# Split products with fewer parts: two of y and h, three of the weights, in a scan followed by a maxout layer

## The chip, the cores and the metric

The kernel runs on one core of a Trainium2 chip. The metric is the device time of one execution in microseconds (us), as the median of several timed runs. A separate execution is recorded by the hardware profiler; it has a time of its own, and its trace is what the views of the profile below are made from. Engines are named as the profile names them: PE is TensorE (PEld its weight loads), DVE is VectorE, ACT is ScalarE, POOL is GpSimd, SP is SyncE, which issues most DMAs.

## The reference

First comes a state-space scan (batch 4, 8 heads, 768 positions, head size 32, state size 16), in chunks. Cut to what matters, for one chunk:

```python
L = exp(cum[i] - cum[j]) * causal                  # decay inside the chunk
y_intra = (C B^T * L) x
y_inter = (C state) * exp(cum)
y = y_intra + y_inter
state = exp(sum(la)) * state + sum_j B_j x_j * exp(cum[-1] - cum[j])
```

Its result is turned into a matrix x of 3072 tokens by 256, and a maxout layer follows, in full float32 accuracy, with weights of 256 x 768 (w1, w2, w3) and 768 x 256 (w_out):

```python
h = maximum(maximum(x @ w1, x @ w2), x @ w3)
out = h @ w_out
```

## The kernel before

**Algebra.** With w2 as a base, the kernel makes the differences d0 = w1 - w2 and d1 = w3 - w2, and uses max(x w1, x w2, x w3) = x w2 + max(0, x d0, x d1). The base is folded ahead of time into one matrix, fold = w2 w_out, so that out = x fold + max(0, x d0, x d1) w_out. An "up" product is x times 128 columns of d0 or d1; a "down" product is 128 rows of h times w_out, or x (called y in the code) times fold.

**Split products.** TensorE multiplies the short type fp32r in one pass, and float32 in several. From block 1 on, each operand is therefore split into fp32r parts, and a product is the sum of three products of parts, accumulated in one PSUM bank, with z = 0, 1, 2 as the index of the term. In the kernel before, every operand has three parts: H (near part: the value times a factor close to 1, rounded), L (far part: made from the difference between the value and H) and S (a crossed part made of H and L). The term z is part z of one operand times part z of the other: H H', L L', S S'. The factors NEAR, RAISE and STRETCH are chosen so that the three add up to the full product.

- For y (`scan_y`): ScalarE writes H from PSUM, VectorE writes L as y - H (step `far`), and VectorE writes S by `crossed`, two steps.
- For h (`halve`, `cross_next`): ScalarE writes H, GpSimd writes L as h - H, and VectorE writes S by `crossed`, one up product later.
- For the weights (`split_steps`), four steps: ScalarE writes H; GpSimd (for fold, which lies in PSUM, VectorE) writes a remainder `rest`; ScalarE casts `rest` into S; VectorE writes L from `rest` and the source. There are ten such splits of 128 x 512 elements: six of d0 and d1 in three column pairs, three of w_out, one of fold.

**Blocks.** The tokens are worked in 6 blocks of 512 (4 batches of 128 positions). For each block the scan makes y by many small matmuls (`scan_old`, line 633, and `scan_own`, line 648), then 12 up products u = 0 to 11 follow (line 802, 6 matmuls of 512 columns each), and the down products (line 926, 24 terms of 4 matmuls of 256 columns). u = 2f takes d0 and u = 2f + 1 takes d1 for the column group f; up product u uses the weight pair q = u // 4. After an even u, ScalarE copies the bank to m; after an odd u, VectorE makes h = max(0, bank, m) (`late`). The up products turn between two PSUM banks, so the next but one waits for that copy or that h. Block 0 is made with the unsplit float32 weights while these are decoded (lines 200 to 215) and the differences are made (line 754).

**Order.** The program is scheduled by hand: each engine runs its instructions in the order in which the code issues them. A word plan gives that order. `OPENING` stands for block 0; then each row of `FIRST`, `STEADY` or `LAST` belongs to one up product. `Z` issues the up product, then the split of the last h (`halve`), then the copy or maximum of the product before (`late`). The other words put work between: `buQ:N` takes N steps from the list of weight splits of pair Q (`paired` interleaves those of d0 and d1), `bo:N` from those of w_out, a number N pops N postponed steps (`later`: score weights, y's parts, state sums), `d` issues one down term, `g` and `G` make the folded matrix (the last `G4` also splits it, all steps at once), `r` is the base product of block 0 (line 907), `t`, `c`, `e`, `s`, `A`, `y`, `X`, `W`, `E` are steps of the next block's scan, with masks on GpSimd (line 476). Thus the plan of block 1 (`FIRST`) carries the weight splits beside the up products that need them: pair 1 from u = 4, pair 2 from u = 8. Output blocks are copied from PSUM into `ob` by ScalarE and VectorE (`put`) and stored by SyncE.

Of the kernel before, what the change touches and what calls it, by code (L numbers as in the profile page):

```python
# [12 lines left out]
F32R = mybir.dt.float32r  # L13
AF = mybir.ActivationFunctionType
ALU = mybir.AluOpType
# [5 lines left out]
def kernel(  # L21
# [20 lines left out]
    nc = tc.nc  # L42

    NB, NH, S, D = x.shape
    N = B.shape[-1]
    P = 128
    NC = S // P
    HN = NH * N
# [6 lines left out]
    KD = DM // P  # L55
    NF = DF // P
    BLK = NB * P
# [3 lines left out]
    HB = BLK // 2  # L61
    Q = P // 2
    NU = NF * 2
    NEAR = 1.0 - 2.0 ** -13
    RAISE = 2.0 ** 12
    STRETCH = 1.0 + 1.0 / RAISE
    NFETCH = 8
    MASKED = -32768.0

# [10 lines left out]
    def half(shape, name, dtype=FP32):  # L80

        return halves.tile(shape, dtype, tag="half", name=name)

    def whole(shape, name, dtype=FP32):

        return wholes.tile(shape, dtype, tag="whole", name=name)

    def plain(t):
        return t.bitcast(FP32)
# [7 lines left out]
    def up_bank(shape, name):  # L97
        return bank("up", 2, shape, name)
# [18 lines left out]
    for k in range(REP):  # L117
        eng = nc.sync if k % 2 == 0 else nc.scalar
# [4 lines left out]
        out=a_sb,  # L123
        in_=a_rows.rearrange("r (c i) -> (r c) i", i=P).rearrange("(w r) i -> r w i", w=2))
# [115 lines left out]
    for _ in range(NFETCH):  # L240
# [7 lines left out]
        out=pick, in_=ident.rearrange("p (r k) -> p k r", k=BH), op=ALU.add, axis=AX.X)  # L248
    npick = const.tile([P, BH], FP32, name="npick")
    nc.vector.tensor_scalar(  # L250
        out=npick, in0=pick, scalar1=-1.0, scalar2=None, op0=ALU.mult)
# [4 lines left out]
        out=hsel, in_=hsel, pattern=[[-N, NH]], compare_op=ALU.is_ge, fill=0.0,  # L256
        base=0, channel_multiplier=1)
    nc.gpsimd.affine_select(
        out=hsel, in_=hsel, pattern=[[N, NH]], compare_op=ALU.is_ge, fill=0.0,
# [3 lines left out]
        out=parity, in_=hsel.rearrange("p (r g) -> p g r", g=2), op=ALU.add, axis=AX.X)  # L263
# [6 lines left out]
        out=mask, in_=mask, pattern=[[1, P]], compare_op=ALU.is_ge, fill=MASKED,  # L270
# [10 lines left out]
        out=ind, in_=by_tile[:, :, :, 0:3].rearrange("p t h q -> p h q t"),  # L281
        op=ALU.add, axis=AX.XY)
# [142 lines left out]
    rest = half([R, 2, P], "sums_rest")  # L425
# [108 lines left out]
    def scan_state(c, kind):  # L534
        st = blocks[c]
        A = kind([HN, NB, 2, D], "A")
        for b in range(NB):
            for r in range(NP):
# [6 lines left out]
                    skip_group_check=True)  # L545
        return lambda: own_state(A, "S", (c + 1, 0))

    def own_state(A, name, key):
        states[key] = to = att.tile([HN, NB, 2, D], FP32, tag="S", bufs=5, name=name)
        nc.vector.tensor_tensor(  # L550
            out=to, in0=A,
            in1=parity.unsqueeze(1).unsqueeze(3).to_broadcast([HN, NB, 2, D]), op=ALU.mult)

    def half_states(c):
# [13 lines left out]
        def add(g):  # L568
            to = (c, 1) if g == 0 else (c + 1, 0)
            own_state(As[g], "S", to)  # L570
            old = att.tile([HN, NB, 2 * D], FP32, tag="old", name="old")
# [98 lines left out]
    y_parts = {}  # L670

    def scan_y(c):

        y_parts[c] = tuple(whole([P, KD, BLK], "y" + n, F32R) for n in "HLS")
        H, L, S = y_parts[c]

        def of(t, k, g):
            return t[:, k].rearrange("p (b g i) -> p b g i", b=NB, g=2)[:, :, g]

        ys = blocks[c]["y"]  # L680
        for k in range(KD):
            for g in range(2):
                nc.scalar.mul(of(H, k, g), ys[k][g], NEAR)

        def far(k):
            for g in range(2):
                nc.vector.tensor_tensor(
                    out=of(L, k, g), in0=ys[k][g], in1=of(plain(H), k, g), op=ALU.subtract)

        steps = [lambda k=k: far(k) for k in range(KD)]  # L690
        return steps + [
            lambda k=k: crossed(S[:, k], plain(H)[:, k], plain(L)[:, k]) for k in range(KD)]

    def crossed(out, H, L):
        nc.vector.scalar_tensor_tensor(  # L695
            out=out, in0=L, scalar=-RAISE, in1=H, op0=ALU.mult, op1=ALU.add)

    h0 = {}

# [28 lines left out]
    up_parts, down_parts, fold_parts = {}, {}, []  # L728

    def split_steps(src, parts):  # L730

        shape = [P, 2, WCOL]
        H, L, S = (half(shape, "w" + n, F32R) for n in "HLS")
        rest = half(shape, "rest")
        parts += [H, L, S]
        eng = nc.gpsimd if src.space != PSUM else nc.vector
        return [
            lambda: nc.scalar.mul(H, src, NEAR * STRETCH),  # L740
            lambda: eng.tensor_tensor(out=rest, in0=src, in1=plain(H), op=ALU.subtract),
            lambda: nc.scalar.copy(out=S, in_=rest),
            lambda: nc.vector.scalar_tensor_tensor(  # L743
                out=L, in0=rest, scalar=RAISE, in1=src, op0=ALU.mult, op1=ALU.add),
        ]

    differences = {}
# [1 line left out]
    def up_steps(q, i):  # L749
        state = {}  # L750

        def differ():
            state["d"] = differences[q, i] = d = half([P, 2, WCOL], "d")
            nc.gpsimd.tensor_tensor(  # L754
                out=d, in0=w_raw[DIFF[i]][q], in1=w_raw[BASE][q], op=ALU.subtract)

        def nth(n):
            def step():
                if n == 0:
                    up_parts[q, i] = []  # L760
                    state["rest"] = split_steps(state["d"], up_parts[q, i])
                state["rest"][n]()
            return step

        return [differ] + [nth(n) for n in range(4)]

    def wo_steps(o):
        state = {}

        def nth(n):  # L770
            def step():
                if n == 0:
                    down_parts[o] = []
                    state["rest"] = split_steps(wo_raw[o], down_parts[o])
                state["rest"][n]()
            return step

        return [nth(n) for n in range(4)]

    def paired(one, two):  # L780
        order = (0, 0, 1, 2, 1, 3, 4, 2, 3, 4)
        which = (0, 1, 0, 0, 1, 0, 0, 1, 1, 1)
        return [(one, two)[w][o] for w, o in zip(which, order)]

    later = []
# [5 lines left out]

    held = {}
    h_parts = {c: {} for c in range(NC)}
    opened, crossings = [], []

    def up(c, u):
        f, i = divmod(u, 2)
        q, g = divmod(f, 2)
        held["up"] = bank = up_bank([P, BLK], "up")
        for z in (0, 1, 2):  # L800
            for k in range(KD):
                nc.tensor.matmul(  # L802
                    out=bank, lhsT=up_parts[q, i][z][:, k, g * P:(g + 1) * P],
                    rhs=y_parts[c][z][:, k], start=(z == 0 and k == 0),
                    stop=(z == 2 and k == KD - 1), skip_group_check=True)
        opened.append((c, u, bank))

    def late():
        if not opened:
            return  # L810
        c, u, up = opened.pop(0)
        f, i = divmod(u, 2)
        if i == 0:
            held["m"] = m = half([P, BLK], "m")
            nc.scalar.copy(out=m, in_=up)  # L815
            cross_next()
            return
        h = half([P, BLK], "h")
        nc.vector.scalar_tensor_tensor(  # L819
            out=h, in0=up, scalar=0.0, in1=held["m"], op0=ALU.max, op1=ALU.max)  # L820
        held["h"] = c, f, h

    def halve():

        if "h" not in held:
            return
        c, f, h = held.pop("h")
        H, L = (half([P, BLK], "h" + n, F32R) for n in "HL")
        h_parts[c][f] = [H, L]
        nc.scalar.mul(H, h, NEAR)  # L830
        nc.gpsimd.tensor_tensor(out=L, in0=h, in1=plain(H), op=ALU.subtract)  # L831
        crossings.append((c, f))

    def cross_next():
        if not crossings:
            return
        c, f = crossings.pop(0)
        H, L = h_parts[c][f]
        S = half([P, BLK], "hS", F32R)
        crossed(S, plain(H), plain(L))  # L840
        h_parts[c][f].append(S)

    based = {"T": [], "turned": 0}

# [72 lines left out]
    def pair_of(c, term, z):  # L917
        kind, n = term
        if kind == "y":
            return y_parts[c][z][:, n], fold_parts[z][:, n]  # L920
        return h_parts[c][n][z], down_parts[n // 2][z][:, n % 2]

    def products(c, o, term, z, bs, first):
        left, right = pair_of(c, term, z)
# [116 lines left out]
    for q in range(NQ):  # L1041
        back["u%d" % q] = paired(up_steps(q, 0), up_steps(q, 1))
# [7 lines left out]
    def first_group(n):  # L1050
# [50 lines left out]
        "Z X0 E bu1:2 E load q",  # L1101
        "Z bu1:2 g q g",
        "Z t bu1:2 g q",
        "Z c e 1 bu1:2 q G4",
        "Z X2 E bu2:2 E G4",
        "Z A 1 1 bu2:2 bo:2 G4",
        "Z s 1 bu2:2 bo:2",
        "Z 1 1 bu2:2 bo:2",
        "Z 1 bo:2 r",
        "Z bo:4 r r",  # L1110
        "Z y 1 r d d 2 d",
        "Z W0 E d 2 E d d",
    ]
    STEADY = [
        "Z t d d load",
# [3 lines left out]
        "Z s d 1 d 1",  # L1119
        "Z d 1 d 1",  # L1120
        "Z d y d 1",
        "Z d 2 d 1",
        "Z d d",
        "Z d d",
        "Z W0 d E d E",
# [70 lines left out]
    for word in OPENING.split():  # L1196
        if word[0] == "n":
            n = int(word[1:])
# [17 lines left out]
    for c in range(1, NC):  # L1216
# [4 lines left out]
        for u in range(NU):  # L1221
            if u == 9 and c < NC - 1:
                queue_downs(c)
            for word in plan[u].split():
# [4 lines left out]
                else:  # L1229
                    act(c, word)  # L1230
    halve()
    cross_next()
    while last:
        last_next()

# [29 lines left out]
```

## Time and profile before

| | us |
|---|---|
| timed runs: median (lowest to highest of 3) | 271.42 (269.75 to 274.23) |
| the profiled execution's own time | 274.01 |
| its span, first to last instruction | 272.3 |
| TensorE matmul busy | 247.8 |
| VectorE / GpSimd / ScalarE busy | 138.6 / 126.2 / 111.4 |

Time bounds of what the trace holds: block 0 and the decoding of the weights until about 70 us, block 1 with the weight splits until about 122 us, blocks 2 to 4 of 35.6 us each, and the last block until 268 us. A view groups instructions by the line of the code, the engine and the tiles by their names, with the count, the busy time, the mean duration of one in ns and the idle time of the engine ahead of them with what ended it. In the view of busy time by stretch each engine's busy time has its number of instructions in brackets, and after the engines come the granted TensorE clock (1.00 is full speed), the DMA share and GB/s. In a wait, the engine and what it was to write stand left of the arrow, and what it waited for right of it; then the sum, the number of waits and the longest.

### The profile page before, as it was taken

The page shows a single profiled execution, that of the slowest core. Times are in us where ns is not written, and L with a number is a line of the kernel's source. Part 1 is how long each engine was busy: PE and PEld are TensorE (multiplying, and loading weights), DVE is VectorE, ACT ScalarE, POOL GpSimd, SP SyncE. Part 2 cuts the span into 40 slices and gives each one's busy share as a digit, 9 for nine tenths or more (in the row PEclk, how much of TensorE's full clock was granted, in tenths as well). Part 3 has the DMA queues.
Part 4 walks back from the last instruction along what each step waited for, and adds up shares of the span by engine and source line. Part 5 has one row for each costly group of instructions (what it writes and reads, how often), then busy time and mean ns, then how long its engine had stood idle before and what let it go on. Part 6 is the DMA issues. An engine that isn't in the chain of part 4 may idle for free.

```text
span 272.3 us, 6712 instructions
## 1 busy us (share of the span) xinstructions
PE 247.8 (91%) x2920; PEld 194.8 (72%) x2920; DVE 138.6 (51%) x214; ACT 111.4 (41%) x208; POOL 126.2 (46%) x118
## 2 busy tenths in 40 slices
PE   6889689497999966979999999999999999999994
PEld 4666245354687844768888888888888888899993
DVE  3494776888618269432544824268243564233222
ACT  4696819303385644325313345123453141222120
POOL 5264457899076785106561373812548121321130
PEclk9999979989999999879999999999999999999999
DMA  7999499997000000119700299000100002002002
GB/s 81 172 356 319 53 185 194 106 93 68 2 0 2 0 2 0 41 43 92 66 2 2 80 79 82 5 2 31 49 0 2 2 5 77 0 2 77 0 2 77
DMA packets 82281, 16.72 MB, mean 61 GB/s; under 512 B 75692, under 2 KB 79180, under 8 KB 82252
## 3 DMA queue, kind: packets, MB, share of 16 engines
q1 hardware_dynamic: 81948, 16.16, 38.1%
q8 instruction: 23, 0.38, 0.6%
q10 hardware_dynamic: 304, 0.13, 0.2%
q14 instruction: 6, 0.05, 0.1%
HBM read 12.99 MB, written 3.29 MB: 60 GB/s over the span
## 4 chain that ended last, share of the span: by engine, by line
PE 70%; DVE 12%; POOL 9%; ACT 3%; issue 3%; DMA 1%; ACTq 0%; POOLq 0%; DVEq 0%
PE up L802 27%; PE o L926 22%; POOL w_u L210 4%; PE y L648 3%; DVE w L215 2%; PE y L633 2%; PE o L907 2%; PE up L1073 2%; PE o L894 2%; DVE w_u L204 2%; PE spread L369 1%; DVE w_u L201 1%; DVE wL L743 1%; PE s L610 1%; DVE yS L695 1%
## 5 line engine op out<-in xcount | busy, mean ns | idle before, releaser
L831 POOL TENSOR_TENSOR hL<-h,hH 128x512 fp32r<-128x512 f32 x30 | 40.0, 1332 | 85.9 <-ACT hH L830 80.5
L695 DVE SCALAR_TENSOR_TENSOR hS<-hL,hH 128x512 fp32r<-128x512 f32 x30 | 26.4, 880 | 52.9 <-POOL hL L831 52.9
L802 PE MATMUL up<-yL,wL 128*128 128x512 f32 x120 | 37.8, 395 | 4.0 <-DVE wL L743 4.0
L830 ACT ACTIVATE hH<-h 128x512 fp32r<-128x512 f32 x30 | 18.9, 631 | 53.6 <-DVE h L819 51.1
L802 PE MATMUL up<-yH,wH 128*128 128x512 f32 x120 | 39.7, 412 | 0.2 <-DVE h L819 0.2
L819 DVE SCALAR_TENSOR_TENSOR h<-up,m 128x512 f32<-128x512 f32 x30 | 20.6, 688 | 37.4 <-PE up L802 36.2
L802 PE MATMUL up<-yS,wS 128*128 128x512 f32 x120 | 37.9, 396 | 0.2
L476 POOL TENSOR_SCALAR_AFFINE_SELECT L<-L 64x1024 f32<-64x1024 f32 x20 | 23.7, 1187 | 17.7 <-ACT L L471 17.0
L815 ACT COPY m<-up 128x512 f32<-128x512 f32 x30 | 17.5, 585 | 31.1 <-PE up L802 27.5
L802 PEld LDWEIGHTS up<-yL,wL 128*128 128x128 f32 x120 | 22.4, 188 | 10.2 <-DVE wL L743 4.8
L802 PEld LDWEIGHTS up<-yS,wS 128*128 128x128 f32 x120 | 22.5, 188 | 5.9 <-DVE yS L695 0.8
L210 POOL TENSOR_TENSOR w_u<-w_u,w_r 128x512 uint32<-128x512 uint32 x12 | 15.2, 1271 | 17.8 <-DVE w_u L204 7.2
L1073 PE MATMUL up<-yT,d 128*128 128x512 f32 x32 | 17.5, 673 | 5.0 <-POOL d L754 3.4
L926 PE MATMUL o<-wH,hH 128*128 128x256 f32 x120 | 21.6, 296 | 0.4 <-ACT ob L912 0.3
L926 PE MATMUL o<-wL,hL 128*128 128x256 f32 x120 | 20.3, 291 | 0.0
L802 PEld LDWEIGHTS up<-yH,wH 128*128 128x128 f32 x120 | 19.1, 191 | 1.6 <-DVE h L819 0.6
L926 PEld LDWEIGHTS o<-wH,hH 128*128 128x128 f32 x120 | 18.0, 194 | 2.8 <-DVE ob L952 0.7
L926 PE MATMUL o<-wS,hS 128*128 128x256 f32 x120 | 19.5, 284 | 0.0
L926 PEld LDWEIGHTS o<-wL,hL 128*128 128x128 f32 x120 | 17.3, 194 | 1.5 <-issue 0.7
L926 PEld LDWEIGHTS o<-wS,hS 128*128 128x128 f32 x120 | 17.1, 191 | 1.1 <-issue 0.5
L1073 PEld LDWEIGHTS up<-yT,d 128*128 128x128 f32 x32 | 6.0, 206 | 11.4 <-issue 5.0
L894 PE MATMUL o<-w,h 128*128 128x256 f32 x48 | 13.8, 409 | 0.1
(139 smaller groups left out, 410.8 us busy)
## 6 DMA issues: line engine op xcount, KB each, us to landing
raw_x<-in_x_dram SPq DMA_DIRECT2D x6, 512.0 KB, 8.5
out_dram<-ob SPq DMA_DIRECT2D x12, 256.0 KB, 2.2
rb<-in_moe_w_dram SPq DMA_DIRECT2D x5, 512.0 KB, 7.1
early<-in_moe_w_dram SPq DMA_DIRECT2D x4, 512.0 KB, 7.1
raw_B<-in_B_dram SPq DMA_DIRECT2D x6, 256.0 KB, 7.4
raw_C<-in_C_dram SPq DMA_DIRECT2D x6, 256.0 KB, 7.1
rb<-in_moe_w_out_dram SPq DMA_DIRECT2D x3, 512.0 KB
right<-sums SPq DMA_DIRECT2D x15, 8.0 KB
```

What stands on the lines that cost most here:

```text
L210: nc.gpsimd.tensor_tensor(out=u, in0=u, in1=r, op=ALU.add)
L476: nc.gpsimd.affine_select(out=part, in_=part, pattern=[[0, 2 * NH], [1, Q]], compare_op=ALU.is_ge, fill=0.0, base=0, channel_multiplier=-1)
L648: nc.tensor.matmul(out=st["y"][t][g][q * D:(q + 1) * D, b], lhsT=st["x"][side(g), b * NH + h], rhs=M[side(g), b, h], start=False, stop=Tru ...
L695: nc.vector.scalar_tensor_tensor(out=out, in0=L, scalar=-RAISE, in1=H, op0=ALU.mult, op1=ALU.add)
L802: nc.tensor.matmul(out=bank, lhsT=up_parts[q, i][z][:, k, g * P:(g + 1) * P], rhs=y_parts[c][z][:, k], start=(z == 0 and k == 0), stop=(z ...
L815: nc.scalar.copy(out=m, in_=up)
L819: nc.vector.scalar_tensor_tensor(out=h, in0=up, scalar=0.0, in1=held["m"], op0=ALU.max, op1=ALU.max)
L830: nc.scalar.mul(H, h, NEAR)
L831: nc.gpsimd.tensor_tensor(out=L, in0=h, in1=plain(H), op=ALU.subtract)
L894: nc.tensor.matmul(out=o[:, i], lhsT=h0[2 * q + g][:, b * P:(b + 1) * P], rhs=wo_raw[q][:, g], start=(i == 0 and q == 0 and g == 0), stop= ...
L926: nc.tensor.matmul(out=o[b // 2][:, b % 2], lhsT=left[:, b * P:(b + 1) * P], rhs=right, start=(first and b % 2 == 0), stop=True, skip_grou ...
L1073: nc.tensor.matmul(out=p, lhsT=of(k), rhs=yT[0][:, k], start=(k == 0), stop=(k == KD - 1))
```

## The change

The weights' parts become H' (the rounded value), L' (the exact difference of the value and H', written in fp32r) and w (the value itself, rounded to fp32r). y and h keep two parts, H and L. The three terms of a product are now H H', H L' and L w: `factor` picks H for z = 0 and 1 and L for z = 2. `crossed`, `cross_next` and the scale factors go, with the crossed parts of y and h, and a weight split has three steps: ScalarE writes H', GpSimd (VectorE for fold) writes L', ScalarE casts the source into w. The lists of steps are shorter, so the words of `FIRST` and `STEADY` are adapted: some `bu` and `bo` counts and pops shrink and some move up by a row. The number of matmuls stays the same.

```diff
@@ scan_y
-        y_parts[c] = tuple(whole([P, KD, BLK], "y" + n, F32R) for n in "HLS")
-        H, L, S = y_parts[c]
+        y_parts[c] = H, L = tuple(whole([P, KD, BLK], "y" + n, F32R) for n in "HL")
...
-                nc.scalar.mul(of(H, k, g), ys[k][g], NEAR)
+                nc.scalar.copy(out=of(H, k, g), in_=ys[k][g])
...
-        steps = [lambda k=k: far(k) for k in range(KD)]
-        return steps + [
-            lambda k=k: crossed(S[:, k], plain(H)[:, k], plain(L)[:, k]) for k in range(KD)]
-
-    def crossed(out, H, L):
-        nc.vector.scalar_tensor_tensor(
-            out=out, in0=L, scalar=-RAISE, in1=H, op0=ALU.mult, op1=ALU.add)
+        return [lambda k=k: far(k) for k in range(KD)]
+
+    def factor(parts, z):
+
+        return parts[z // 2]
@@ split_steps
-        H, L, S = (half(shape, "w" + n, F32R) for n in "HLS")
-        rest = half(shape, "rest")
-        parts += [H, L, S]
+        H, L, W = (half(shape, "w" + n, F32R) for n in "HLW")
+        parts += [H, L, W]
         eng = nc.gpsimd if src.space != PSUM else nc.vector
         return [
-            lambda: nc.scalar.mul(H, src, NEAR * STRETCH),
-            lambda: eng.tensor_tensor(out=rest, in0=src, in1=plain(H), op=ALU.subtract),
-            lambda: nc.scalar.copy(out=S, in_=rest),
-            lambda: nc.vector.scalar_tensor_tensor(
-                out=L, in0=rest, scalar=RAISE, in1=src, op0=ALU.mult, op1=ALU.add),
+            lambda: nc.scalar.copy(out=H, in_=src),
+            lambda: eng.tensor_tensor(out=L, in0=src, in1=plain(H), op=ALU.subtract),
+            lambda: nc.scalar.copy(out=W, in_=src),
         ]
@@ paired
-        order = (0, 0, 1, 2, 1, 3, 4, 2, 3, 4)
-        which = (0, 1, 0, 0, 1, 0, 0, 1, 1, 1)
+        order = (0, 0, 1, 2, 1, 2, 3, 3)
+        which = (0, 1, 0, 0, 1, 1, 0, 1)
@@ up
-                    rhs=y_parts[c][z][:, k], start=(z == 0 and k == 0),
+                    rhs=factor(y_parts[c], z)[:, k], start=(z == 0 and k == 0),
@@ late
             nc.scalar.copy(out=m, in_=up)
-            cross_next()
@@ halve
-        nc.scalar.mul(H, h, NEAR)
+        nc.scalar.copy(out=H, in_=h)
         nc.gpsimd.tensor_tensor(out=L, in0=h, in1=plain(H), op=ALU.subtract)
-        crossings.append((c, f))
-
-    def cross_next():
-        if not crossings:
-            return
-        c, f = crossings.pop(0)
-        H, L = h_parts[c][f]
-        S = half([P, BLK], "hS", F32R)
-        crossed(S, plain(H), plain(L))
-        h_parts[c][f].append(S)
@@ pair_of
-            return y_parts[c][z][:, n], fold_parts[z][:, n]
-        return h_parts[c][n][z], down_parts[n // 2][z][:, n % 2]
+            return factor(y_parts[c], z)[:, n], fold_parts[z][:, n]
+        return factor(h_parts[c][n], z), down_parts[n // 2][z][:, n % 2]
@@ FIRST
-        "Z c e 1 bu1:2 q G4",
+        "Z c e 1 bu2:2 q G4",
         "Z X2 E bu2:2 E G4",
         "Z A 1 1 bu2:2 bo:2 G4",
-        "Z s 1 bu2:2 bo:2",
-        "Z 1 1 bu2:2 bo:2",
-        "Z 1 bo:2 r",
-        "Z bo:4 r r",
-        "Z y 1 r d d 2 d",
-        "Z W0 E d 2 E d d",
+        "Z s 1 bo:2",
+        "Z 1 1 bo:2",
+        "Z 1 bo:1 r",
+        "Z bo:2 r r",
+        "Z y 1 r d d 1 d",
+        "Z W0 E d E d d",
@@ STEADY
-        "Z d 2 d 1",
+        "Z d 1 d",
```

More of the change, by code (lines that the diff above doesn't have):

```diff
@@ L63 @@
     NU = NF * 2
-    NEAR = 1.0 - 2.0 ** -13
-    RAISE = 2.0 ** 12
-    STRETCH = 1.0 + 1.0 / RAISE
     NFETCH = 8
@@ L763, in nth @@
             return step
-        return [differ] + [nth(n) for n in range(4)]
+        return [differ] + [nth(n) for n in range(3)]
     def wo_steps(o):
@@ L776, in nth @@
             return step
-        return [nth(n) for n in range(4)]
+        return [nth(n) for n in range(3)]
     def paired(one, two):
-        order = (0, 0, 1, 2, 1, 3, 4, 2, 3, 4)
-        which = (0, 1, 0, 0, 1, 0, 0, 1, 1, 1)
+        order = (0, 0, 1, 2, 1, 2, 3, 3)
+        which = (0, 1, 0, 0, 1, 1, 0, 1)
         return [(one, two)[w][o] for w, o in zip(which, order)]
@@ L793 @@
     h_parts = {c: {} for c in range(NC)}
-    opened, crossings = [], []
+    opened = []
     def up(c, u):
@@ L1231 @@
     halve()
-    cross_next()
     while last:
```

## The prediction

> **What bounds the kernel now.** I read the page first, for the busy shares and the slices.
>
> ```profile
> span 272.3 us, 6712 instructions
> PE 247.8 (91%) x2920; PEld 194.8 (72%) x2920; DVE 138.6 (51%) x214; ACT 111.4 (41%) x208; POOL 126.2 (46%) x118
> PE   6889689497999966979999999999999999999994
> ```
>
> TensorE is busy 91% of the span, and 21 slices in a row, up to the last, are nines. The change takes no matmul away: every split product still has three terms. So it can only pay where TensorE stands still or runs at half clock, and next I asked for busy times by stage.
>
> ```profile
> core 0: us, PE busy (x) PEld busy (x) DVE busy (x) ACT busy (x) POOL busy (x), PEclk, DMA share, GB/s
> 0.00:65.50 65.50, 52.28 (x448) 30.90 (x448) 45.29 (x79) 35.72 (x66) 41.67 (x45) 0.95 1.04 169
> 65.50:71.50 6.00, 5.98 (x203) 4.43 (x204) 4.40 (x6) 1.94 (x5) 2.96 (x3) 1.00 0.02 5
> 71.50:95.80 24.30, 24.10 (x181) 18.27 (x179) 10.81 (x17) 15.26 (x29) 14.66 (x13) 1.00 0.00 1
> 95.80:111.15 15.35, 10.66 (x95) 7.56 (x95) 12.71 (x15) 7.21 (x13) 8.80 (x7) 0.89 0.00 1
> 111.15:121.40 10.25, 7.99 (x213) 6.51 (x212) 2.81 (x6) 2.56 (x7) 1.29 (x1) 0.83 0.14 48
> 121.40:268.30 146.90, 146.76 (x1787) 127.15 (x1786) 61.86 (x93) 48.68 (x90) 56.80 (x50) 1.00 0.24 31
> 268.30:272.30 4.00, 0.00 (x0) 0.00 (x0) 0.69 (x1) 0.00 (x0) 0.00 (x0) 0.91 0.39 131
> ```
>
> From 121.4 to 268.3 us TensorE is idle for 0.14 us of 146.9, at full clock. Whatever VectorE does less there, the stage keeps its length, but for one small wait below. Before 65.5 us the kernel decodes weights and makes block 0, which the change does not touch until its end. What is left is 65.5 to 121.4 us: block 1, while the weights are being split. Its worst part, 95.8 to 111.15, has 4.7 us without a matmul, and VectorE is the busiest engine in it, 12.71 of 15.35 us. The waits say who holds TensorE there.
>
> ```profile
> PE up L802 <- DVE wL L743: 4.0, 2, 2.1
> PE y L648 <- issue: 2.0, 1, 2.0
> PEld o L926 <- DVE ob L952: 0.7, 3, 0.3
> PE s L589 <- DVE wL L743: 0.5, 1, 0.5
> PE up L802 <- DVE h L819: 0.2, 1, 0.2
> ```
>
> Three of the five rows name wL or h, both on VectorE in that stretch; wL is the weights' far part, which the change makes on another engine.
>
> **The change part by part.** These groups show what leaves VectorE.
>
> ```profile
> L695 DVE SCALAR_TENSOR_TENSOR hS<-hL,hH 128x512 fp32r<-128x512 f32 x30 | 26.4, 880 | 52.9 <-POOL hL L831 52.9
> L695 DVE SCALAR_TENSOR_TENSOR yS<-yL,yH 128x512 fp32r<-128x512 f32 x10 | 9.8, 1012 | 0.0
> L743 DVE SCALAR_TENSOR_TENSOR wL<-rest,d 128x512 fp32r<-128x512 f32 x6 | 7.0, 1164 | 0.6 <-POOL rest L741 0.6
> L743 DVE SCALAR_TENSOR_TENSOR wL<-rest,w 128x512 fp32r<-128x512 f32 x3 | 3.1, 1042 | 0.0
> L741 POOL TENSOR_TENSOR rest<-d,wH 128x512 f32<-128x512 f32 x6 | 8.1, 1357 | 9.8 <-ACT wH L740 9.8
> L742 ACT CAST wS<-rest 128x512 fp32r<-128x512 f32 x10 | 6.2, 619 | 5.4 <-POOL rest L741 4.6 <-DVE rest L741 0.8
> ```
>
> VectorE loses 30 crossings of h (26.4 us), 10 of y (9.8) and, with one of 0.7 for the folded product, ten wL (10.8): 47 us, so 138.6 becomes about 92. GpSimd keeps its nine subtractions; they write wL itself instead of a remainder. ScalarE keeps its casts, now of the source instead of the remainder, so they no longer wait 4.6 us for GpSimd. Scaled copies become plain ones: 619 ns a cast against 631 to 634 for the scaled forms, nothing. Where this touches TensorE there are five terms.
>
> *Opening of block 1, 0.8 us.* The first up product waits for y's parts in turn.
>
> ```profile
> 70.81 1.21 ACT L683 ACTIVATE yH<-y 128x256 fp32r<-128x256 f32 x4 [2.92 <-PE y L648]
> 71.22 1.42 DVE L687 TENSOR_TENSOR yL<-y,yH 128x256 fp32r<-128x256 f32 x4 [1.01 <-ACT yH L683]
> 72.41 0.79 PE L802 MATMUL up<-yL,wL 128*128 128x512 f32 x2
> 73.90 0.19 PEld L802 LDWEIGHTS up<-yS,wS 128*128 128x128 f32 x1 [0.42 <-DVE yS L695]
> 75.80 1.39 PE up L802 x6
> ```
>
> Six up matmuls take 1.39 us when nothing holds them, 0.23 each. The third starts at 72.41 now and can again; terms one and two then need only yH (there by 72.02), and the third term yL, whose last piece ends at 72.64. So the sixth starts at 72.41 + 3 x 0.23 = 73.1 instead of 73.9. ScalarE has a fourth weight cast ahead of yH, but stands idle 2.92 us there. Without that cover a cast would cost 0.6.
>
> *Scores, 0.5 us.* The score matmuls wait for the bank of the folded product, which wL reads last. Its VectorE subtraction stays, the second VectorE pass goes, and the cast reads the bank beside the subtraction. Between 0 and 0.5; I take 0.5.
>
> *Waits for wL and h, 4.2 us.* These are the two products that stop after their first term.
>
> ```profile
> 101.94 1.77 DVE L743 SCALAR_TENSOR_TENSOR wL<-rest,w 128x512 fp32r<-128x512 f32 x1
> 102.06 0.73 PE L802 MATMUL up<-yL,wL 128*128 128x512 f32 x2 [2.12 <-DVE wL L743]
> 104.36 0.73 PE L802 MATMUL up<-yH,wH 128*128 128x512 f32 x2 [0.24 <-DVE h L819]
> 106.92 0.74 PE L802 MATMUL up<-yL,wL 128*128 128x512 f32 x2 [1.83 <-DVE wL L743]
> 89.91 1.29 POOL L741 TENSOR_TENSOR rest<-d,wH 128x512 f32<-128x512 f32 x1 [2.17 <-ACT wH L740]
> ```
>
> VectorE runs hS, a score weight and wL in program order, and this wL takes 1.77 us, against 1.16 in the mean. After the change the first of these two wL is a GpSimd subtraction listed one plan row ahead of the one at 89.91, the second takes the place of that one and ends near 91.2. On GpSimd the second stands ahead of the masks and state sums of that time, and an hL queued behind the first moves by up to 1.3 us; only down products after 118 us read it. TensorE stood ready for the first wL at 102.06 - 2.12 = 99.94, and comes 1.3 us earlier: needed near 98.6, so about 7 us of slack cover both. 2.12 + 0.24 + 1.83 = 4.2; were the slack gone, this term would be zero.
>
> *Half clock, 1.7 us.* These windows lie on the grid of the clock's changes.
>
> ```profile
> 100.90:104.32 3.42, 2.06 (x8) 1.43 (x8) 3.42 (x5) 0.54 (x2) 1.64 (x1) 1.00 0.00 0
> 104.32:107.73 3.41, 1.54 (x5) 0.97 (x6) 3.41 (x4) 2.15 (x4) 2.43 (x2) 1.00 0.00 0
> 107.73:111.14 3.41, 3.41 (x9) 2.65 (x8) 3.23 (x5) 1.65 (x3) 0.28 (x1) 0.50 0.00 0
> 114.56:117.97 3.41, 1.45 (x91) 1.17 (x75) 0.76 (x2) 0.96 (x4) 0.00 (x0) 1.00 0.00 0
> 117.97:121.38 3.41, 3.11 (x12) 2.54 (x11) 1.35 (x3) 0.94 (x3) 0.00 (x0) 0.50 0.18 60
> ```
>
> A window with 1.54 or 1.45 us of matmul is followed by one at 0.50; the one with 2.06 is not. The window 107.73 to 111.14 is full of work at half clock, and half of its 3.41 us is lost, 1.7. Without the waits the window before it is full, and this goes (0 if a gap remains). The one at 117.97 follows the stall of 2.0 us in the block's scan, which has no releaser in the program; I leave both standing.
>
> The Trainium skill ("TensorE: Matmul & The Clock Gate", What's actually happening) says the clock halves after an idle window of about 3.4 us. By that rule gaps of 2.1 and 1.8 us would halve nothing, this term would be 0 and the sum 6.2. Here 1.9 us of idling in the window were enough.
>
> *Output copies, 0.7 us.* Once in each of blocks 2 to 4 the down products wait for the output copy ob on VectorE.
>
> ```profile
> 188.99 0.68 DVE L695 SCALAR_TENSOR_TENSOR hS<-hL,hH 128x512 fp32r<-128x512 f32 x1
> 189.59 0.68 DVE L952 COPY ob<-o 128x512 f32<-128x512 f32 x1
> ```
>
> ob is queued behind hS, which goes. The waits give 0.7 in all; the stage's idle time gives 0.14 as the lower end, since modelled ends cover short gaps. I take 0.7.
>
> The plan's fewer words move no matmul, load or DMA; SyncE's queue keeps its order. The end gains nothing: TensorE is full to 268.3, and the last ob and its store take the same 4.0 us.
>
> Sum: 0.8 + 0.5 + 4.2 + 1.7 + 0.7 = 7.9 us. The profiled execution took 274.01 us, 1.7 over its span of 272.3, and so would take 266.1 with a span of 264.4. It is 2.6 above the median of the timed runs, 271.42; taken off the median the sum gives 263.5.
>
> **The rivals.** Two per cent, about what a measurement of this kernel tells from no change, lies at 266.0 and 276.8.
>
> *The half clock stays* although the waits go, because halving takes more than 1.9 us of idling and something else set it at 107.7: 271.4 - 6.2 = 265.2. Against it: of the windows shown, both with under 1.6 us of matmul are followed by 0.50. Chance 0.08. The rule of the Trainium skill quoted above (TensorE: Matmul & The Clock Gate) would have it so.
>
> *A new wait takes wL's place* in 95.8 to 111.15: GpSimd's wL or ScalarE's casts come late, or h does. Then 4.2 and 1.7 are lost in part or whole: 266 to 271.4 - 2.0 = 269.4. For it: GpSimd is busy 8.80 of 15.35 us there and ScalarE 7.21. Against it: both subtractions end before 92 us. Chance 0.10.
>
> *The change frees VectorE but no path*, every wait being replaced by one as long: 271.4. The nines speak for it after 121 us, the named waits against it before. Chance 0.05.
>
> *The stall in the scan goes as well*, should instructions reach TensorE in better step: 2.0 and the second half clock, 1.7, give 259.8. Chance 0.08.
>
> *Slower: instruction supply.* The page's queues show how TensorE is fed.
>
> ```profile
> q8 instruction: 23, 0.38, 0.6%
> ```
>
> 23 packets of about 16 KB carry 2 x 2920 instructions, some 254 in each; a scan runs 384 within 2.5 us, and once, at 115.3, TensorE outran its supply for 2.0 us. If the shift in time, or a few wait instructions fewer, puts a packet's border so in the four other scans, each costs 2.0 + 1.7 = 3.7: 271.4 - 7.9 + 14.8 = 278.3. From three extra stalls on (11.1) the change loses. For it: the one stall. Against: the matmul stream is the same, so borders hardly move. Chance 0.07. The Trainium skill ("Runtime: NRT & Kernel Launch", Instruction fetch mechanics) states blocks of 256 instructions whose cost is mostly hidden; the packets agree, the 2.0 us do not.
>
> **How the numbers follow.** The forecast has the remaining 0.62 and its own range is 261.5 to 266.0: 1.7 less gain if the timed runs had no half clock at 107 us, 2 more if the second one goes alone. Faster by over 2%: 0.62 + 0.08 + 0.08 = 0.78; within: 0.10 + 0.05 = 0.15; slower: 0.07. The range of 8 in 10 reaches down to the vanished stall, 259.5, and up over half of the new-wait case, 268.0; left out are 0.05 + 0.05 + 0.07.
>
> **What would show it.** VectorE near 92 us with no hS, yS or wL from two operands; the first up product without waits after yH; no wait of the up products for wL; one half-clock window after 60 us instead of two; ob behind nothing; 121 to 268 us of the trace of before shorter by at most 0.7. A wait of the up products for GpSimd or ScalarE, or a second idle stretch named issue, would make it wrong.

## The result, and the profile after

The kernel after takes 262.81 us in the median, the kernel before 272.83 us (four runs of each, beside one another). The ratio is 0.971 with a 95% interval of 0.964 to 0.978: faster. Forecast were 263.5 us and a gain of 7.9 us; the two medians differ by 10.0.

In some executions block 0 has three more windows at half clock and ends 2 to 6 us later; the ratios leave out only those over 1.5% above the kernel's quickest, so the traces are compared below from the first up product of block 1 to the end of the last matmul.

The page of the kernel after, and its busy times by stretch (the bounds are the same points of the program as in the table of before):

```profile
span 261.1 us, 6670 instructions
PE 242.3 (93%) x2920; PEld 192.7 (74%) x2920; DVE 94.6 (36%) x164; ACT 110.4 (42%) x208; POOL 123.8 (47%) x118
```

```profile
0.00:64.85 64.85, 52.25 (x448) 30.89 (x448) 45.29 (x79) 35.73 (x66) 41.65 (x45) 0.92 1.06 171
64.85:70.85 6.00, 5.99 (x203) 4.44 (x204) 2.17 (x4) 2.36 (x6) 2.97 (x3) 1.00 0.02 5
70.85:94.25 23.40, 23.40 (x180) 18.27 (x179) 5.19 (x11) 15.00 (x29) 15.14 (x15) 1.00 0.00 1
94.25:102.70 8.45, 8.13 (x95) 6.66 (x95) 3.99 (x7) 5.75 (x11) 6.98 (x6) 1.00 0.01 2
102.70:111.12 8.42, 6.60 (x212) 5.40 (x211) 1.51 (x4) 3.17 (x8) 1.29 (x1) 1.00 0.10 35
111.12:257.10 145.98, 145.96 (x1788) 127.08 (x1786) 35.80 (x61) 48.38 (x90) 55.74 (x50) 1.00 0.24 33
```

VectorE went from 138.6 to 94.6 us (near 92 was forecast), 50 instructions fewer; TensorE has its 2920 matmuls still. The stretch that took 15.35 us takes 8.45, with 8.13 us of matmul and no half clock. The long stretch behind it became only 0.9 us shorter. The waits of TensorE that are left in block 1, in the view of who waited for whom (sum, times, longest):

```profile
PE y L645 <- issue: 1.4, 1, 1.4
PE o L906 <- ACT ob L892: 0.4, 1, 0.4
PE s L586 <- ACT wW L735: 0.3, 1, 0.3
```

No up product waits for wL or h any more. From the first up product to the last matmul the profiled execution of before took 196.7 us, that of after 186.2: 10.6 us less, 2.7 more than forecast. A second trace of each, below, shows which of the two was the odd one.

### The profile page after: what moved, and what is told of

It is laid out like the page before. It is cut to its first block, busy times and chain, and to the rows that moved or that the text cites. A ratio compares the mean times of both kernels' runs of the same rounds, so it can differ in the third digit from the quotient of the medians.

```text
span 261.1 us, 6670 instructions
## 1 busy us (share of the span) xinstructions
PE 242.3 (93%) x2920; PEld 192.7 (74%) x2920; DVE 94.6 (36%) x164; ACT 110.4 (42%) x208; POOL 123.8 (47%) x118
## 4 chain that ended last, share of the span: by engine, by line
PE 76%; DVE 9%; POOL 6%; DMA 4%; issue 2%; ACT 2%; ACTq 0%; POOLq 0%; DVEq 0%
PE up L793 31%; PE o L906 23%; POOL w_u L207 4%; DMA sums<-hl 3%; DVE w L212 3%; PE y L645 3%; DVE w_u L201 2%; PE o L874 2%; PE fold L846 2%; PE y L630 2%; DVE w_u L198 2%; PE s L586 2%; PE spread L366 1%; PE o L887 1%; PE A L558 1%
## 5 line engine op out<-in xcount | busy, mean ns | idle before, releaser
L820 ACT CAST hH<-h 128x512 fp32r<-128x512 f32 x30 | 18.6, 620 | 51.0 <-DVE h L809 51.0
L793 PE MATMUL up<-yH,wL 128*128 128x512 f32 x120 | 37.4, 392 | 0.0
L793 PE MATMUL up<-yL,wW 128*128 128x512 f32 x120 | 37.2, 391 | 0.0
L793 PEld LDWEIGHTS up<-yH,wL 128*128 128x128 f32 x120 | 22.5, 188 | 5.2
L793 PEld LDWEIGHTS up<-yL,wW 128*128 128x128 f32 x120 | 22.5, 188 | 5.1
L906 PE MATMUL o<-wL,hH 128*128 128x256 f32 x120 | 20.0, 288 | 0.0
L906 PE MATMUL o<-wW,hL 128*128 128x256 f32 x120 | 19.5, 284 | 0.0
L906 PEld LDWEIGHTS o<-wL,hH 128*128 128x128 f32 x120 | 16.9, 190 | 1.5 <-issue 0.7
L906 PEld LDWEIGHTS o<-wW,hL 128*128 128x128 f32 x120 | 17.1, 190 | 1.1 <-issue 0.5
L595 DVE TENSOR_TENSOR L<-s,L 128x512 f32<-128x512 f32 x20 | 12.8, 683 | 9.3 <-PE s L586 9.3
L1053 PEld LDWEIGHTS up<-yT,d 128*128 128x128 f32 x32 | 6.2, 213 | 10.6 <-issue 5.2
```

What stands on the lines that cost most here:

```text
L595: nc.vector.tensor_tensor(out=M, in0=s.rearrange("p b h i -> p b (h i)"), in1=M, op=ALU.mult)
L793: nc.tensor.matmul(out=bank, lhsT=up_parts[q, i][z][:, k, g * P:(g + 1) * P], rhs=factor(y_parts[c], z)[:, k], start=(z == 0 and k == 0), ...
L820: nc.scalar.copy(out=H, in_=h)
L906: nc.tensor.matmul(out=o[b // 2][:, b % 2], lhsT=left[:, b * P:(b + 1) * P], rhs=right, start=(first and b % 2 == 0), stop=True, skip_grou ...
L1053: nc.tensor.matmul(out=p, lhsT=of(k), rhs=yT[0][:, k], start=(k == 0), stop=(k == KD - 1))
```

## The experiments

All kernels start from the kernel after, but for the second trace of before. "Stage" is the time from the first up product of block 1 to the end of the last matmul in the trace, "half clock" the number of windows at 0.50 within it.

| kernel | stage, us | half clock | quickest execution, us | ratio to before |
|---|---|---|---|---|
| before, two traces | 196.7; 193.2 | 2; 1 | 269.5 | |
| after, two traces | 186.2; 186.2 | 0; 0 | 262.6 | 0.971 [0.964, 0.978] |
| passes over h back | 187.3 | 0 | 264.0 | 0.974 [0.964, 0.984] |
| passes over h and y back, two traces | 190.8; 188.6 | 1; 0 | 267.4 | 0.994 [0.990, 0.999] |
| wL on VectorE, old rows | 190.1 | 0 | 266.5 | 0.983 [0.973, 0.993] |
| old rows only | 187.8 | 1 | 263.2 | 0.972 [0.961, 0.984] |
| scan cut in two | 185.0; 185.2 | 0; 0 | 261.6 | 0.974 [0.963, 0.986]; 0.962 [0.955, 0.968] |
| 128 more instructions | 189.3 | 0 | 265.6 | 0.984 [0.978, 0.989] |
| bank copies held up | 194.6 | 1 | 277.0, timed once | |
| cut scan and two small moves | 183.8 | 0 | 260.5 | 0.960 [0.953, 0.967] |

**The passes over h put back.**

```diff
         nc.gpsimd.tensor_tensor(out=L, in0=h, in1=plain(H), op=ALU.subtract)
+        crossings.append((c, f))
...
+    def crossed(out, H, L):
+        nc.vector.scalar_tensor_tensor(
+            out=out, in0=H, scalar=0.0, in1=L, op0=ALU.mult, op1=ALU.add)
```

> The kernel after, with the 30 VectorE passes over h put back in their old place (an up product later) as L = 0 x H + L, and the third term reading that copy; the result is the same. Theory (the gain is waits of block 1, VectorE's time from block 2 on is covered): the output copy's wait returns, 0.3 us in each of three blocks, and little in block 1: 263.0 to 264.8 us. Rival (VectorE's time pays wherever it is taken away; these are 26 of its 47 us): more than half of the gain goes, 267 us or more.

The stage grew by 1.2 us, the quickest execution by 1.4: in the range of the theory, far from the rival. But not where it was expected. Blocks 2 to 4 keep the period of the kernel after (35.26 us for the first of them in both), so hS alone does not hold the output copy up. The cost stands in block 1: up product 9 waits 0.6 us for h, which follows hS on VectorE, and from the start of up product 7 to that of 10 it takes 0.9 us longer; another 0.35 lies at the end of block 1, where the stretch without a releaser took 1.7 us instead of 1.4. VectorE and GpSimd of that stretch, then the product that waits:

```profile
98.12 1.76 DVE L693 SCALAR_TENSOR_TENSOR hS<-hH,hL 128x512 fp32r<-128x512 f32 x1 [3.20 <-POOL hL L826]
99.81 0.68 DVE L595 TENSOR_TENSOR L<-s,L 128x512 f32<-128x512 f32 x1
100.41 0.68 DVE L814 SCALAR_TENSOR_TENSOR h<-up,m 128x512 f32<-128x512 f32 x1
```

```profile
98.04 1.30 POOL L738 TENSOR_TENSOR wL<-w,wH 128x512 fp32r<-128x512 f32 x1
```

```profile
101.14 0.73 PE L797 MATMUL up<-yH,wH 128*128 128x512 f32 x2 [0.64 <-DVE h L814]
```

hS takes 1.76 us instead of 0.68, and ends about 0.5 us after GpSimd's subtraction does. The Trainium skill ("SBUF — State Buffer", Who interferes with whom) says that a VectorE instruction with two SBUF inputs contends with a GpSimd one that reads SBUF; the row agrees. All but one of the passes that the change removes read two SBUF operands (wL of the folded product reads one in PSUM). In the traces of before and after from block 1 on, h and the score weights, which read one input from PSUM, take 0.67 to 0.69 us whether GpSimd works beside them or not.

**The passes over h and y put back**, for what the weights' split gives alone.

```diff
+            lambda k=k: crossed(S[:, k], plain(H)[:, k], plain(L)[:, k]) for k in range(KD)]
```

> As the one before, and the 10 VectorE passes over y put back as well, with the old pop counts: the old kernel's VectorE work but for the weights' split. Theory: another 0.8 to 0.9 us at the first up product of block 1, nothing elsewhere: 263.9 to 265.8. Rival (VectorE's time pays): 36 of 47 us are back, so some three quarters of the gain are gone, 269 us or more.

Neither bound held by the quickest execution, 267.4 us, which lies between the theory and the rival. The ratio lies on the rival's side (269 us is 0.986 of the 272.8 of before): the ten executions run up to 271.6 us, and where those without a trace lost their time isn't known. The trace adds to the wait for h two things. The first up product waits for yS again, 0.9 us from the first up product to the second. And the output copies wait, by this row of the waits:

```profile
PEld o L925 <- DVE ob L951: 0.8, 3, 0.3
```

The queue in block 3 of this kernel shows what stands ahead of the copy:

```profile
180.07 2.38 DVE L695 SCALAR_TENSOR_TENSOR yS<-yH,yL 128x512 fp32r<-128x512 f32 x2
182.38 0.68 DVE L695 SCALAR_TENSOR_TENSOR hS<-hH,hL 128x512 fp32r<-128x512 f32 x1
182.98 0.68 DVE L951 COPY ob<-o 128x512 f32<-128x512 f32 x1
```

It is the two yS passes, 2.38 us with GpSimd's hL (180.28 to 181.90) beside the first of them, that make hS and ob late. The rest of the stage's 4.6 us is a stretch without a releaser that grew from 1.38 to 1.82 us, and a half-clock window behind it. The second trace, with none of the two:

> The kernel after with the VectorE passes over h and y put back, unchanged, for a second trace: 190.8 us from the first up product to the last matmul in the first one, with one half-clock window. Theory: 189 us without a half-clock window, 190.8 with one; the waits for yS, h and ob are there again (0.9, 0.6 and three times 0.3 us). Rival: a wait that the first trace did not have.

It took 188.6 us, without a half-clock window, with the same waits for yS, h and ob and no new one. So the passes over h and y cost 2.5 us by their waits, and 4.6 where a longer stretch without a releaser and the half clock come on top.

**wL on VectorE, in the old rows of the plan.**

```diff
-            lambda: eng.tensor_tensor(out=L, in0=src, in1=plain(H), op=ALU.subtract),
+            lambda: eng.tensor_tensor(out=rest, in0=src, in1=plain(H), op=ALU.subtract),
             lambda: nc.scalar.copy(out=W, in_=src),
+            lambda: nc.vector.scalar_tensor_tensor(
+                out=L, in0=src, scalar=0.0, in1=rest, op0=ALU.mult, op1=ALU.add),
```

> The kernel after, with the weights split in four steps and the old rows of the plan: GpSimd writes the remainder, VectorE makes wL of it (0 x source + remainder). No passes over h or y. Theory as predicted (wL's place on VectorE and in the plan made the waits): up products 8 and 9 of block 1 wait 2 to 4 us for wL again and a half-clock window may follow: 265.5 to 270. Rival (wL was late because it stood behind the passes over h on VectorE): without those the waits stay under 1 us: 262.8 to 264.5.

The stage grew by 3.9 us, the quickest execution by 3.9. These are its waits, and VectorE's queue at those of the up products (the rows `wL<-d` are the ones waited for, `wL<-w` is a weight of w_out):

```profile
PE up L796 <- DVE wL L737: 2.1, 2, 1.9
PE s L586 <- DVE wL L737: 1.1, 1, 1.1
```

```profile
97.22 1.73 DVE L737 SCALAR_TENSOR_TENSOR wL<-d,rest 128x512 fp32r<-128x512 f32 x1
98.87 1.77 DVE L737 SCALAR_TENSOR_TENSOR wL<-w,rest 128x512 fp32r<-128x512 f32 x1
100.56 0.68 DVE L812 SCALAR_TENSOR_TENSOR h<-up,m 128x512 f32<-128x512 f32 x1
101.17 1.27 DVE L595 TENSOR_TENSOR L<-s,L 128x512 f32<-128x512 f32 x2
102.36 1.48 DVE L737 SCALAR_TENSOR_TENSOR wL<-d,rest 128x512 fp32r<-128x512 f32 x1
```

The theory holds in sum, the rival in one half: without hS ahead of it the first wL is 0.3 us late instead of 2.1, the second 1.9 instead of 1.8. So the first wait of the kernel before was hS and wL in one queue; the second comes without hS too, from wL's place behind the wL of w_out, h and the score weights.

**The old rows only.**

```diff
-        "Z c e 1 bu2:2 q G4",
+        "Z c e 1 bu1:2 q G4",
...
+        "Z s 1 bu2:2 bo:2",
+        "Z 1 1 bu2:2 bo:2",
+        "Z 1 bo:2 r",
+        "Z bo:4 r r",
```

> The kernel after, with only the rows of the plan for the weight splits of block 1 as before (pair 2 begins a row later, w_out's steps stand as before). Theory (who makes wL matters, not the row): within 0.5 us of the kernel after, 262.3 to 263.3, no wait of an up product over 0.3 us. Rival (the earlier row pays): up products 8 and 9 wait for wL, 265 us or more.

The quickest execution took 263.2 us and no up product waits for a weight part: who makes wL decides, not the row. The stage is 1.6 us longer by one half-clock window, which belongs to the next question.

**The clock.** Three up-bank copies were held up by idle ScalarE copies.

```diff
+    IDLE = {2: 5, 3: 7, 4: 8}
...
+            if u == 8 and c in IDLE:
+                spare = half([P, BLK], "spare")
+                for _ in range(IDLE[c]):
+                    nc.scalar.copy(out=spare, in_=based["first"].rearrange("p k m -> p (k m)"))
```

> The kernel after, with 5, 7 and 8 idle copies of ScalarE (about 0.55 us each, into a tile that nobody reads) put ahead of the bank copy of up product 8 in blocks 2, 3 and 4: up product 10 waits for that bank. With 1.6 us of slack by the rows (1.39 of the next up product and 0.95 of down products, less 0.74 for the copy) TensorE should stand still about 1.1, 2.2 and 2.8 us, each after a long stretch without a gap. Theory (the clock halves for 3.41 us when about half a window of 3.41 us, 1.7, was idle): no half clock after the first, half clock after the third, and after the second if it lies within one window; each costs up to 1.7 us: 269.0 + 1.7 to 3.4 = 270.7 to 272.4. Rival (the rule that a whole window must be idle): none of the three halves anything, 269.0.

TensorE stood still for 0.85, 2.16 and 2.86 us (it met the wait at the down products, through their output copy on ScalarE, not at up product 10). The windows of the clock's grid around the second and the third:

```profile
183.83:187.24 3.41, 2.70 (x16) 2.06 (x14) 0.69 (x1) 3.25 (x6) 0.78 (x1) 1.00 0.00 0
187.24:190.66 3.42, 1.98 (x12) 1.81 (x13) 0.69 (x1) 2.01 (x4) 0.95 (x1) 1.00 0.31 108
190.66:194.07 3.41, 3.41 (x22) 2.57 (x21) 0.00 (x0) 1.57 (x3) 1.45 (x2) 1.00 0.13 45
224.79:228.20 3.41, 1.12 (x9) 1.12 (x10) 0.69 (x1) 2.83 (x5) 0.20 (x1) 1.00 0.07 24
228.20:231.61 3.41, 3.41 (x12) 2.86 (x12) 0.00 (x0) 0.59 (x1) 1.07 (x1) 0.50 0.37 130
```

The gap of 2.16 us fell across a border, 0.7 and 1.4 us, and halved nothing; of that of 2.86 us 2.3 lay in one window, and the next ran at 0.50. This kernel was timed once only, so its total is not used. The nearest cases on either side are the windows at the end of block 1, with the old rows:

```profile
107.41:110.82 3.41, 1.69 (x21) 1.29 (x21) 1.51 (x4) 1.86 (x5) 0.00 (x0) 1.00 0.02 5
110.82:114.23 3.41, 3.41 (x13) 3.22 (x14) 0.00 (x0) 0.00 (x0) 0.00 (x0) 0.50 0.29 88
```

and in the kernel after:

```profile
106.51:109.92 3.41, 1.97 (x53) 1.41 (x34) 1.51 (x4) 1.55 (x5) 0.00 (x0) 1.00 0.02 5
109.92:113.33 3.41, 3.02 (x20) 2.36 (x20) 0.08 (x1) 0.33 (x1) 0.00 (x0) 1.00 0.26 84
```

Here 1.69 us of matmul was too little and 1.97 enough: about half of the 3.41 us. The rival, a whole idle window, falls.

**The stretch without a releaser**, in the scan at the end of block 1. First the run of fast instructions was cut; `yo` is `scan_old` alone, `yw` is `scan_own` and `scan_y`:

```diff
-        "Z bo:2 r r",
-        "Z y 1 r d d 1 d",
+        "Z bo:2 r r yo",
+        "Z yw 1 r d d 1 d",
```

> The kernel after, with the scan of block 2 cut in two: its first 64 matmuls (from the old state) move ahead of up product 10 of block 1, so that 12 slow instructions of TensorE stand inside the run of 384 fast ones. Theory (the stretch of 1.4 us without a releaser in that scan is TensorE outrunning its supply of instructions): it shrinks to under 0.4 us, and the time falls by 0.8 to 1.8 us, to 261.0 to 262.0. Rival (the stretch is something in the scan's data or banks): it stays near 1.4 us and the time at 262.3 to 263.2.

The stretch went (1.38 us in the kernel after, under 0.15 in this trace, 0.19 in a second one) and the stage fell by 1.1 us. Then the borders of the packets were moved:

```diff
-        for b in range(NB):
+        for b in 2 * list(range(NB)) if c == 1 else range(NB):
```

> The kernel after, with the 64 small state matmuls of block 1, made while block 0 runs, issued twice (the same values written again): 128 more instructions of TensorE, so that the borders of its instruction packets fall 128 places earlier in every later scan. Theory of the instruction supply (a packet of 256 used up within a scan stalls): the stretch in the scan at the end of block 1 goes, and one of 1.4 to 2.2 us appears in the scans of blocks 2, 3 and 4 each, with or without half clock after it: 262.8 + 0.9 - 1.4 + 3 x 1.4 to 3 x 3.7 = 266.5 to 273. Rival (borders don't matter): only the pad's own 0.9 us, 263.2 to 264.2, and the stretch stays where it was.

Block 1's scan ran through, and blocks 2, 3 and 4 stood still in theirs, 1.25, 1.49 and 1.39 us. Two of the three, and the sum, in the timeline and the waits of that kernel:

```profile
136.79 0.62 PE L645 MATMUL y<-L,raw_x 64*32 64x64 f32 x36 [1.25 <-issue]
173.83 0.54 PE L645 MATMUL y<-L,raw_x 64*32 64x64 f32 x34 [1.49 <-issue]
```

```profile
PE y L645 <- issue: 4.1, 3, 1.5
```

The stage grew by 3.1 us and the quickest execution by 2.9, a little under the theory's range, since no gap reached 1.7 us and no half clock followed. The rival, that borders don't matter, falls.

The traces also hold the fetching of the instructions, in packets of 16 KB. In each of the ten other traces that show the stretch, it ends behind the same 2217 matmuls and weight loads. In the padded kernel the three end behind 3237, 4257 and 5277, so these places are always 1020 apart, or 1024, four times 256, with TensorE's other instructions counted. Each stretch ends 1.4 to 1.6 us after a packet has landed. By this count TensorE entered the packet ahead (255 matmuls and loads earlier) in the kernel after at 105.15 us and had used it up by 106.85; the next one was fetched from 105.86 to 106.79 and in use at 108.23. So the next packet took 3.1 us to come, where the scan uses one up in 1.7; the 1.4 us of slower work in the cut scan make up the difference.

**The two kernels compared again, and a quicker one.** The kernel after and the one with the cut scan ran once more in common rounds, beside a third with two further moves: the last base product of block 0 one row earlier, and w of the folded product cast from the SBUF copy.

```diff
-        "Z bo:2 r r",
-        "Z y 1 r d d 1 d",
+        "Z bo:2 r r r yo",
+        "Z yw 1 d d 1 d",
...
-            lambda: nc.scalar.copy(out=W, in_=src),
+            lambda: nc.scalar.copy(out=W, in_=src if copy is None else copy),
...
-            for step in split_steps(based["sum"], fold_parts):
+            for step in split_steps(based["sum"], fold_parts, based["first"]):
```

> The kernel after, unchanged, on the same chip and in the same rounds as the two kernels with the cut scan, to compare them with. Expected: 262.6 to 262.9 us in its quickest executions, a ratio to the kernel before near 0.97.

> The kernel with the cut scan again, beside the kernel after. Theory of the instruction supply: 1.1 us below the kernel after, as its trace shows from the first up product on (185.0 against 186.2 us). Rival (the gain is given back elsewhere, or the chip's spread hides it): no difference, within 0.4 us.

> The kernel after with three small moves: the scan of block 2 cut in two as in the run with the cut scan; the last base product of block 0 moved up by one up product, so that its output copy is done before the down products need the bank; and the near-source part w of the folded product cast from the copy of it in SBUF instead of its PSUM bank. Expected from the traces: 1.1 us from the cut, 0.44 from the bank wait, 0.3 from the scores' wait, 1.8 us less between the first up product and the last matmul than in the kernel after (186.2 us there): 184.4. Rival (the earlier base product only moves the wait, or the stretch without releaser comes back, since the slow instructions it took out of the scan no longer stand in it): 185.0 or more.

The kernel after gave a stage of 186.2 us again and 0.973 [0.966, 0.980]; the cut scan 185.2 us and 0.962 [0.955, 0.968]; the third 183.8 us and 0.960 [0.953, 0.967], better than the 184.4 us expected. From its first up product to its last matmul the profile shows next to no idle time of TensorE:

```profile
76.50:260.35 183.85, 183.80 (x2270) 157.25 (x2268) 46.35 (x83) 72.12 (x137) 79.12 (x71) 1.00 0.18 28
```

Its quickest execution, 260.5 us, is 2.2 us under that of the kernel after. The intervals of the three ratios overlap; that the cut scan is quicker is shown by the traces and the quickest executions, 1.0 us, not by its ratio alone.

**The kernel before again.**

> The kernel before, unchanged, for a second trace of it. From the first up product to the last matmul it took 196.7 us in the first trace, with two half-clock windows (after the waits for wL, and after the stretch without releaser), 1.7 us each. Theory (the waits are the program's, the half clock hangs on where the free-running windows fall): the same waits for wL within 0.3 us, and 193 to 197 us in steps of about 1.7 by the number of half-clock windows. Rival (the first trace was an outlier in its waits too): waits for wL under 3 us in all, or over 5.

The stage took 193.2 us, with one half-clock window. The waits:

```profile
PE up L802 <- DVE wL L743: 2.9, 2, 2.1
PE s L589 <- DVE wL L743: 0.5, 1, 0.5
PE y L648 <- issue: 1.3, 1, 1.3
```

By the letter the rival's bound of 3 us was met, 2.9. The windows show why:

```profile
98.66:102.07 3.41, 1.28 (x6) 0.76 (x5) 3.41 (x4) 1.15 (x2) 2.15 (x2) 1.00 0.00 0
102.07:105.49 3.42, 3.38 (x9) 2.10 (x7) 3.42 (x5) 1.84 (x4) 1.53 (x2) 0.50 0.00 0
```

Here the first wait of 2.1 us fell within one window. The half clock came before the second wait and ran into it: TensorE was slow while wL was being made, and waited 0.8 us instead of 1.8. Half clock and a wait that follow each other do not add up.

## Why the prediction was right

The change is faster by what was named, and the time was met within 0.7 us: 263.5 forecast, 262.8 measured. That it fits so closely is in part luck: the median of before moved from 271.4 to 272.8 us with one more execution, and the gain is 10.0 us between the medians but 6.9 between the quickest executions. The terms, between the same points in the traces (first and second trace of before, against after):

| term | forecast, us | measured, us |
|---|---|---|
| first to second up product | 0.8 | 0.9; 0.9 |
| scores, up product 6 to 7 | 0.5 | 0.2; 0.2 |
| waits for wL and h, with the half clock, up product 7 to 10 | 4.2 + 1.7 | 6.7; 5.0 |
| end of block 1, up product 10 to 12 | 0 | 1.8; -0.1 |
| blocks 2 to 5, output copies | 0.7 | 1.0; 1.0 |
| sum | 7.9 | 10.6; 7.0 |

*Opening.* The step held: after the change the second and third terms follow without a gap, and yH alone delays the second matmul. The passes over y put back cost the same 0.9.

*Scores.* This term was too large, and its reason wrong. "The cast reads the bank beside the subtraction": it does not. ScalarE's cast of w waits 0.8 us for VectorE's wL, which reads the same bank, and the scores wait for the cast:

```profile
L735 ACT CAST wW<-fold 128x512 fp32r<-128x512 f32 x1 | 0.6, 586 | 0.8 <-DVE wL L734 0.8
```

One pass took the other's place. With the cast reading the SBUF copy, in the quickest kernel, the scores wait no more.

*Waits for wL and h.* The step held, and the old rows showed that the 7 us of slack were not needed from the earlier row: wL on GpSimd is in time in either. The working misread one row: the wL of 1.77 us at 101.94 is one of w_out and was only beginning when the first wait ended. The one waited for took 0.67 us and came late because of what stood ahead of it:

```profile
99.06 1.75 DVE L695 SCALAR_TENSOR_TENSOR hS<-hL,hH 128x512 fp32r<-128x512 f32 x1 [2.42 <-POOL hL L831]
100.73 0.68 DVE L598 TENSOR_TENSOR L<-s,L 128x512 f32<-128x512 f32 x1
101.34 0.67 DVE L743 SCALAR_TENSOR_TENSOR wL<-rest,d 128x512 fp32r<-128x512 f32 x1
```

So hS and wL made the first wait together, which the working did not separate. From the start of up product 7 to that of 10, hS alone cost 0.9 us (its row: a wait of 0.6 for h) and wL alone 3.2 (its rows: 0.3 and 1.9 for wL, 0.2 for h); the rows come out lower because modelled ends of matmuls cover a part of each gap. The kernel before, with both, lost 6.7 and 5.0 there.

*Half clock.* It went with the waits, as the rows had it and against the rule of the Trainium skill ("TensorE: Matmul & The Clock Gate", What's actually happening), whose sum lay at 6.2. Adding its 1.7 us to the full waits was right for the first trace only: in the second the window covers part of a wait.

*Output copies.* The size held roughly, 1.0 for 0.7 (and for the 0.7 that the prediction named as the most that the stage from 121 us on would lose), with the reason amiss: "ob is queued behind hS, which goes". With hS back alone no block got longer; yS ahead of both is what makes ob late.

*What was left standing.* "I leave both standing" was said of the stall in the scan and the half clock after it. In the first trace of before they were 1.96 us and one window, in its second 1.28 and none, in the kernel after 1.38 and none. The packet of instructions that ended the stall took 1.43 us to fetch in that first trace and 0.93 in the other two. These 1.8 us are the chance of that one trace and no part of the change. So the first pair of traces overstates the gain, and the second, 7.0 us, is near the 6.9 between the quickest executions (269.5 and 262.6). It is also why no half-clock window is left, where the prediction's signs had one.

*The slower rival.* Its mechanism was shown by the padded kernel: borders of instruction packets that fall into a scan stop TensorE. Its price was too high, 1.25 to 1.49 us each instead of 3.7, for no half clock followed; the change did not move the borders, since the matmul stream is the same and the stall ends behind the same 2217 matmuls and loads before and after.

One thing stays open in part. By the second traces the weights' split gives 4.5 us (193.2 to 188.6) and the passes over h and y 2.5. By the quickest executions it is the other way round, 2.1 (269.5 to 267.4) and 4.8. But the execution of 267.4 us is the traced one with the half-clock window, whose stage is 2.2 us longer than that of the second trace; less these, the shares would be 4.3 and 2.6. How many windows at half clock an untraced execution had isn't known.

## What to carry to other kernels

Where the busiest engine is already full, look for the stretch in which it is not, and price an edit by the waits in that stretch: of 44 us taken from VectorE, 7 came back. A pass in an in-order queue can be nearly in time alone (0.3 us late here) and 2.1 us late behind one more, so look at what stands ahead of it, and first at passes that read two SBUF operands while GpSimd works (up to 1.77 us here instead of 0.68). Before a half-clock window is added to a sum, check with a second trace that it is the program's and not that execution's.

## What was not expected of the hardware

From block 1 on, the clock of TensorE was halved for a window of 3.41 us after a window of the same grid with 1.69 us of matmul or less, and not with 1.97 or more; between them the cases are mixed (1.72 not, 1.76 yes, 1.83 not). In block 0, with other shapes of matmul, busy time alone does not tell: two of the traces halve the clock after a window with more of it, 2.39 and 2.47 us. This is the first, in the kernel with the cut scan:

```profile
13.01:16.43 3.42, 2.39 (x52) 1.69 (x46) 3.39 (x7) 3.42 (x8) 2.56 (x3) 1.00 1.14 295
16.43:19.84 3.41, 2.71 (x37) 1.83 (x34) 2.19 (x5) 1.33 (x4) 1.97 (x1) 0.50 1.05 388
```

What the halving goes by there isn't shown. A gap of 2.16 us across a border halved nothing, and the wait of 2.1 us for wL halved it in the trace in which it lay within one window, not in that in which it lay across a border.

TensorE's instructions come in packets of some 256, and a scan of 384 instructions in about 2.5 us can use one up before the next is there: 1.25 to 1.96 us of standing still. Twelve slower instructions in the midst of the scan (1.4 us of work) were enough to hide it.
